# A gated linear attention with an MLP on one core: seven block products for eight in the last eight chunks, one mask instruction per visit, fewer TensorE waits, and a new instruction order

## The chip, the cores and the metric

The kernel runs on one core of a Trainium2 chip. The metric is the device time of one execution in microseconds (us); lower is better. The engines named below are PE (TensorE matmuls; PEld is its weight load), DVE (VectorE), ACT (ScalarE), POOL (GpSimd) and SP (SyncE, which issues every DMA here).

## What is computed

The attention part is a recurrence over 768 tokens for 4 batches and 8 heads of width 48. Its state is a 48x48 complex matrix per head, turned and damped at every token. The MLP takes the 3072 tokens of width 384 (8 heads by 48) through 2048 features with a parametric ReLU and back to 384.

```python
mag = np.sqrt(a_re * a_re + a_im * a_im)
scale = np.minimum(mag, 0.999) / (mag + 1e-06)
a_re_n, a_im_n = (a_re * scale, a_im * scale)
for t in range(S):
    new_re = ar * S_re - ai * S_im
    new_im = ar * S_im + ai * S_re
    kv = np.einsum('bhd,bhe->bhde', k[:, :, t], v[:, :, t])
    S_re, S_im = (new_re + kv, new_im)
    y[:, :, t] = np.einsum('bhd,bhde->bhe', q[:, :, t], S_re)
...
h = x @ w_in
g = np.maximum(h, 0.0) + alpha * np.minimum(h, 0.0)
return (g @ w_out).astype(np.float32)
```

All arithmetic that matters here is fp32. The two weight matrices arrive as 64-bit words and are turned into fp32 on the chip.

## The kernel before, in words

**Chunks and units.** The tokens are cut into 24 chunks of 128 (6 per batch). One chunk of attention is a *unit* (`unit`). For each unit the 8 heads are handled together, with 96 partitions (48 values, real and imaginary).

**Gates.** `gates` turns a_re and a_im into what the units need: the decays (`decs` in DRAM, read back as the tile `T`) and the phases (`phs` in DRAM, read back as `PP`). The phases are a running complex product over tokens, done in three levels: wide products of 8 steps (lines L338 and L340 with 576 and 288 elements), a block level with 72 and 36 elements, and a serial scan over blocks (12 and 6 elements), which starts from a `carry` of the group before. The narrow instructions (80 elements or less, and the ones after the scan, L396 to L411) run on `tiny_engine`: DVE for batch 0, GpSimd for the others. The last step spreads the scan's results over all tokens (L426 and L429 on DVE), and then the phases are sent. There are nine gate groups: chunk 0; chunks 1 and 2; chunks 3 to 5 of batch 0; and two groups of three chunks for each other batch. Three chunks make instructions of 1152 elements on 128 partitions.

**A unit.** DVE turns keys and queries by the phases (L661, L663). Then come three *visits* of two levels each, (1, 2), (4, 8) and (16, 32). At each level DVE scales one half by the decays (L717, "KQ step"), ACT copies what the next level will overwrite (L740, L756), PE forms key-query products of 32x32 blocks in PSUM (`ps_lv`, L678, 16 matmuls per level), and the products are masked into the tiles `A1` to `A32` (DVE at L702 for levels 1, 2, 4 and 8, one instruction per level; ACT at L699 for 16 and 32). After the visits PE transposes the keys (L785), forms the key-value sums (`ps_kv`, L797), multiplies the masked products by the values (`ps_y`, L817), and adds the part that comes from the state (L841). DVE carries the state on (L826, L829). ACT copies the output out, and it goes through DRAM (`ysc`) to become `xT`, the MLP's input.

**The MLP.** Chunks are taken in 14 groups of 1, 1, 2 (ten times), 1 and 1 chunks. `features` makes 128 of the 2048 features (16 rounds, f) for a group: 3 matmuls into one of two `ps_h` buffers (L889; 256 moving columns for two chunks, 128 for one), ACT's negated ReLU (L896), then one DVE instruction that joins the slopes (L898); that instruction frees the `ps_h` buffer. `outputs` multiplies a chunk's 128 features by 128 rows of w_out (L908, 384 moving columns, 16 matmuls per chunk accumulated in `ps_o`), ACT copies the sum out (L918), and SP stores it.

**The weights.** 16 pieces are loaded and converted by ACT, POOL (L515) and DVE (L517, L519) in the first part of the run.

**The order.** Every engine takes its instructions in program order, and the program order is written out by hand: `ORDER` is a string of letters, each of which lets one task (a gate group, a unit, the loads, the MLP) run to its next `yield`. The letters A to I are the gate groups, then come the loads, the weights, the 24 units, the loads of `xT` and the MLP. The numbers inside the `yield`s are costs that the writer of the string used; at run time they do nothing. Waits between engines are semaphores that the framework places from the tiles that are written and read.

## Time and profile before

| | us |
|---|---|
| median of 3 runs | 838.61 (837.79 to 839.77) |
| the profiled execution | 836.36 |
| its span, first to last instruction | 834.6 |
| PE busy | 695.8 |
| DVE busy | 651.7 |
| ACT busy | 438.7 |
| POOL busy | 200.6 |

The profile's table of stages gives for each stretch of the span the busy time of each engine, with the number of records in brackets. An fp32 matmul leaves two records, so 768 records at L908 are 384 matmuls. "Busy" of PE counts overlapping records once. The granted clock in such a table is TensorE's, as a share of full speed. The groups table gives, for a line, engine and shape, the number of records, the busy time, and the mean duration of one in ns.

### The profile page before, as it was taken

The page shows a single profiled execution, that of the slowest core. Times are in us where ns is not written, and L with a number is a line of the kernel's source. Part 1 is how long each engine was busy: PE and PEld are TensorE (multiplying, and loading weights), DVE is VectorE, ACT ScalarE, POOL GpSimd, SP SyncE. Part 2 cuts the span into 40 slices and gives each one's busy share as a digit, 9 for nine tenths or more (in the row PEclk, how much of TensorE's full clock was granted, in tenths as well). Part 3 has the DMA queues.
Part 4 walks back from the last instruction along what each step waited for, and adds up shares of the span by engine and source line. Part 5 has one row for each costly group of instructions (what it writes and reads, how often), then busy time and mean ns, then how long its engine had stood idle before and what let it go on. Part 6 is the DMA issues. An engine that isn't in the chain of part 4 may idle for free.

```text
span 834.6 us, 26848 instructions
## 1 busy us (share of the span) xinstructions
PE 695.8 (83%) x11488; PEld 527.7 (63%) x11488; DVE 651.7 (78%) x1020; ACT 438.7 (53%) x937; POOL 200.6 (24%) x293
## 2 busy tenths in 40 slices
PE   0001435889998999899999999999999999999998
PEld 0001424667776777677777777777777777777776
DVE  5989999999997899889988988979767652644112
ACT  7758787467635665565657446644344342323221
POOL 5231222328603600360135103330341000000000
PEclk9999755899999999999999999999999999999999
DMA  6696977786478579737873586457834832511110
GB/s 195 189 280 157 274 170 227 217 220 175 100 222 209 145 171 248 186 88 197 233 194 77 158 259 159 115 143 216 210 99 118 202 70 61 136 34 43 35 30 10
DMA packets 194174, 130.91 MB, mean 157 GB/s; under 512 B 74120, under 2 KB 185864, under 8 KB 194056
## 3 DMA queue, kind: packets, MB, share of 16 engines
q1 hardware_dynamic: 194056, 129.20, 58.8%
q8 instruction: 90, 1.47, 0.7%
q14 instruction: 28, 0.23, 0.1%
HBM read 100.82 MB, written 35.71 MB: 164 GB/s over the span
## 4 chain that ended last, share of the span: by engine, by line
PE 53%; DVE 23%; DMA 12%; POOL 4%; issue 4%; ACT 4%; SPq 1%; DVEq 0%; ACTq 0%; POOLq 0%
PE ps_o L908 22%; PE ps_h L889 20%; DVE KQ L717 4%; DMA T<-decs 4%; PE ps_lv L678 4%; DVE gate L426 3%; DVE gate L338 2%; PE ps_y L817 2%; DMA phs<-gate 2%; PE ps_y L841 2%; PE ps_kv L797 2%; DVE gate L429 2%; DMA g_sb<-in_w_out_dram 1%; POOL gate L338 1%; DVE gate L340 1%
## 5 line engine op out<-in xcount | busy, mean ns | idle before, releaser
L889 PE MATMUL ps_h<-xT,w_in_sb 128*128 128x256 f32 (+1 forms) x1344 | 297.3, 355 | 9.0 <-DMA xT<-ysc 7.0
L908 PE MATMUL ps_o<-w_out_sb,g_sb 128*128 128x384 f32 x768 | 297.2, 500 | 7.9 <-DVE g_sb L898 4.5
L889 PEld LDWEIGHTS ps_h<-xT,w_in_sb 128*128 128x128 f32 x1344 | 235.7, 194 | 82.1 <-DMA xT<-ysc 7.8
L898 DVE SCALAR_TENSOR_TENSOR g_sb<-g_sb,al,ps_h 128x256 f32<-128x256 f32 (+1 forms) x224 | 97.5, 436 | 117.9 <-ACT g_sb L896 117.6
L896 ACT ACTIVATE g_sb<-ps_h 128x256 f32<-128x256 f32 (+1 forms) x224 | 78.8, 352 | 200.7 <-PE ps_h L889 199.4
L908 PEld LDWEIGHTS ps_o<-w_out_sb,g_sb 128*128 128x128 f32 x768 | 136.5, 191 | 59.4 <-DVE g_sb L898 7.0
L717 DVE TENSOR_TENSOR KQ<-KQ,T 96x1024 f32<-96x1024 f32 x120 | 149.2, 1246 | 23.8 <-PE ps_lv L678 15.2
L678 PE MATMUL ps_lv<-WQ 96*32 96x32 f32 x2304 | 34.3, 204 | 72.6 <-DVE WQ L661 56.2
L678 PEld LDWEIGHTS ps_lv<-WQ 96*32 96x32 f32 x2304 | 26.5, 116 | 92.7 <-DVE WQ L661 56.2
L740 ACT COPY WQ<-KQ 96x1024 f32<-96x1024 f32 x48 | 49.9, 1040 | 22.2 <-DVE KQ L717 22.2
L338 POOL TENSOR_TENSOR gate<-gate 128x72 f32<-128x72 f32 x42 | 25.8, 615 | 134.3 <-ACT gate L368 131.5
L515 POOL TENSOR_SCALAR top<-top 128x768 f32<-128x768 f32 x16 | 41.2, 2578 | 65.2 <-ACT top L507 65.1
L756 ACT COPY W<-KQ 96x512 f32<-96x512 f32 x48 | 30.9, 644 | 40.1 <-DVE KQ L717 30.3
L338 DVE TENSOR_TENSOR gate<-gate 128x576 f32<-128x576 f32 (+5 forms) x84 | 48.6, 579 | 3.8 <-ACT gate L368 2.4
L855 ACT COPY T<-ps_y 48x256 f32<-48x256 f32 x96 | 31.6, 365 | 34.5 <-PE ps_y L841 33.7
L817 PE MATMUL ps_y<-A,VL 64*48 64x64 f32 x2304 | 42.0, 224 | 4.4 <-issue 3.8
L426 DVE TENSOR_TENSOR gate<-gate 128x1152 f32<-128x1152 f32 (+2 forms) x36 | 43.6, 1235 | 0.1
L817 PEld LDWEIGHTS ps_y<-A,VL 64*48 64x48 f32 x2304 | 39.7, 125 | 5.4 <-issue 4.5
L699 ACT ACTIVATE A<-ps_lv,columns 128x64 f32<-128x64 f32 x144 | 37.6, 334 | 9.2 <-PE ps_lv L678 9.1
L678 PE MATMUL ps_lv<-KQ,W 96*32 96x32 f32 x1536 | 24.5, 203 | 20.3 <-ACT W L756 19.7
L702 DVE TENSOR_TENSOR A<-ps_lv,mask 128x256 f32<-128x256 f32 x96 | 37.6, 412 | 0.0
L717 DVE TENSOR_TENSOR KQ<-WQ,T 96x1024 f32<-96x1024 f32 x24 | 29.5, 1231 | 6.4 <-DMA T<-decs 4.2
(106 smaller groups left out, 899.4 us busy)
## 6 DMA issues: line engine op xcount, KB each, us to landing
T<-decs SPq DMA_DIRECT2D x48, 384.0 KB
PP<-phs SPq DMA_DIRECT2D x24, 387.0 KB
KQ<-in_q_dram SPq DMA_DIRECT2D x48, 192.0 KB
decs<-gate SPq DMA_DIRECT2D x7, 1152.0 KB
phs<-gate SPq DMA_DIRECT2D x14, 576.0 KB
KQ<-in_k_dram SPq DMA_DIRECT2D x40, 192.0 KB
vsc<-in_v_dram SPq DMA_DIRECT2D x48, 144.0 KB
VL<-vsc SPq DMA_DIRECT2D x24, 288.0 KB
```

What stands on the lines that cost most here:

```text
L338: on(4 * k).tensor_tensor(out=m, in0=w[:, 1::-1].unsqueeze(2).to_broadcast([P, 2, 2, k]), in1=pairs_of(u), op=ALU.mult)
L426: TT(out=m[:, a], in0=U5[:, 1 + a], in1=turned(off3, o)[:, a].unsqueeze(1).unsqueeze(3).to_broadcast([P, L // 2, nb, 2]), op=ALU.mult)
L515: nc.gpsimd.tensor_scalar(out=top, in0=top, scalar1=F64_SMALL, scalar2=None, op0=ALU.max)
L678: nc.tensor.matmul(t[64 * i + j:64 * i + j + HC // 2, p], lhsT=keys(n, g), rhs=queries(n, g), start=True, stop=True)
L699: nc.scalar.activation(a[:, :, cols], t[:, :, at:at + name], AF.Copy, scale=s)
L717: nc.vector.tensor_tensor(out=x, in0=x if x0 is None else x0, in1=m, op=ALU.mult)
L740: nc.scalar.copy(z.rearrange("p i n t -> p i (n t)").rearrange("p i (m h) -> p m i h", h=h), bass.AP(tensor=KQ.tensor, offset=KQ.offset + ...
L817: nc.tensor.matmul(o, lhsT=Vp[h][64 * i:64 * i + 64, s, e_ * D:(e_ + 1) * D], rhs=a, start=False, stop=False)
L889: nc.tensor.matmul(p, lhsT=w_in_sb[:, f // 2, kk, f % 2 * P:(f % 2 + 1) * P], rhs=x_of[m][:, kk], start=(kk == 0), stop=(kk == NK - 1))
L896: nc.scalar.activation(gt, p, AF.Relu, scale=-1.0)
L898: nc.vector.scalar_tensor_tensor(out=gt, in0=gt, scalar=al_1[:, f:f + 1], in1=p, op0=ALU.mult, op1=ALU.add)
L908: nc.tensor.matmul(sums[0], lhsT=gt[:, c * P:(c + 1) * P], rhs=w_out_sb[:, f], start=(f == 0), stop=(f == NF - 1))
```

## The change

Six things are changed at once.

1. **Gate groups.** Batch 0 has two groups of three chunks instead of three groups (1, 2 and 3 chunks); and only the very first group keeps its narrow instructions on DVE. Those of chunks 3 to 5 move to GpSimd.
2. **Masks.** The masks of two levels lie side by side, and one DVE instruction of 512 elements per visit replaces two of 256. The tiles of levels 4 and 8 have one buffer instead of two.
3. **Waits.** The PSUM tiles `misc` and `lv` are allocated once and handed round by hand, and matmuls that read KQ or T, or write these tiles, are declared free of dependency on the loads of KQ and T. In the built program PE waits for 775 semaphores instead of 888.
4. **Output products.** For the last eight chunks, in four pairs, the product of features (2 chunks by 2048) and w_out (2048 by 384) is cut into 2x2 blocks and formed from 7 block products instead of 8. Each product is a *group* of 8 matmuls with 192 moving columns. The extra work is sums of blocks of w_out, made once (`more`: 8 DVE instructions of 768 elements), sums of blocks of features (per pair `sides`: 6 DVE instructions, and `fourth`: 2, of 512 elements), and the joining of the seven results (`plus`: 7 DVE instructions of 192 elements per pair, and one ACT copy). ACT's 16 copies of 384 elements at L918 fall away for these chunks. Space comes from the two gate buffers after the gates are done. The last pair is made of the last two groups of one chunk each.
5. **MLP order.** Features of the last five groups are interleaved with these groups of matmuls instead of with `outputs`.
6. **ORDER** is another string.

```diff
-    "AABAMMAAAAAAAAAAAAAAAAAMAAAAAMABJMNAJNNABNAAAAAAAAAAAAANKJKAKBKNBAABAAAABABBJAAAALAAAAAAABAMAAAAOKAK"
+    "AAAAAAALALLALABAAABJAMIAIIIMAMMAAALKLJAMAALAMMKKNAAAJANAAAAJANAAAAAAAJJAJAAJMMAJAAAJNNNAJNNAAAAJALAN"
...
+    def turned(i):
+        tc.declare_no_dep(i.ins, group="load", reason="the engine that this waits for has written all of it since")
...
-        tiny, tiny_engine = (DVE, nc.vector) if b == 0 else (POOL, nc.gpsimd)
+        tiny, tiny_engine = (DVE, nc.vector) if g == 0 else (POOL, nc.gpsimd)
...
+        def mask_both(name, t, e):
+            e = yield DVE(2 * HP * HC, e, takes=(R[name],))
+            a = work.tile([P, 2, HP, HC], F32, tag=f"A{name}", name=f"A{name}", bufs=2 if name == 1 else 1)
+            k = LEVELS.index(name)
+            whole = [P, 2, HP, 2, HC // 2]
+            nc.vector.tensor_tensor(out=a.rearrange("p a n (g t) -> p a n g t", g=2), in0=t.unsqueeze(3).to_broadcast(whole),
+                                    in1=both_masks[:, k:k + 2].rearrange("p a (g t) -> p a g t", g=2).unsqueeze(2).to_broadcast(whole),
+                                    op=ALU.mult)
...
+    def more():
+        T1, T2, T4 = [z[:, i * n:(i + 1) * n].rearrange("p (f e) -> p f e", f=NH) for i in range(3)]
+        held["T"] = [B11, T2, B12, T4, B21, T1, B22]
+        for dst, a, b in ((T1, B12, B11), (T2, B22, T1), (T4, B21, T2)):
+            for f in range(0, NH, 4):
+                nc.vector.tensor_tensor(out=dst[:, f:f + 4], in0=a[:, f:f + 4], in1=b[:, f:f + 4], op=ALU.subtract)
...
+    def sides(m, r):
+        A11, S2, A21, A22, A12, S1, _ = held[m]
+        for dst, a, b, op in ((S1, A21, A22, ALU.add), (A21, A11, A21, ALU.subtract), (S2, S1, A11, ALU.subtract)):
+            for f in range(0, NH, 4):
+                r = yield DVE(4 * P, r)
+                nc.vector.tensor_tensor(out=dst[:, f:f + 4], in0=a[:, f:f + 4], in1=b[:, f:f + 4], op=op)
+        return r
...
+    def group(m, j, r, tag="o"):
+        for k in range(NH):
+            nc.tensor.matmul(z, lhsT=held[m][j][:, k], rhs=held["T"][j][:, k], start=k == 0, stop=k == NH - 1)
...
+    def plus(dst, z, u, *e, takes=()):
+        t = yield DVE(DH, *e, takes=takes)
+        nc.vector.scalar_tensor_tensor(out=dst, in0=z, scalar=scale, in1=u, op0=ALU.mult, op1=ALU.add)
...
+        if alone:
+            yield from second()
+            yield "need", m + 1, NF - 1
+        r = yield from sides(m, made[m + alone, NF - 1][1])
+        yield "pause"
+        z, e = yield from group(m, 1, [t1, r], o)
+        t2 = yield from plus(u2, z, u1, e, t1)
...
-    GATES = [(0, 0, 1), (0, 1, 3), (0, 3, 6)] + [(b, c, c + 3) for b in range(1, B) for c in (0, 3)]
+    GATES = [(0, 0, 3), (0, 3, 6)] + [(b, c, c + 3) for b in range(1, B) for c in (0, 3)]
```

In the diff, `alone` is true for the last pair.

## The prediction, made before the changed kernel had run

> **What bounds the kernel now.** I read the table of stages first (start:end, length, busy time of PE, PEld, DVE, ACT and POOL, granted clock, share of the DMA engines, GB/s):

> ```profile
> 0.00:60.00 60.00, 0.66 (x32) 0.52 (x32) 46.59 (x138) 39.34 (x62) 24.60 (x38) 1.00 0.79 218
> 60.00:180.00 120.00, 59.20 (x1394) 48.27 (x1395) 117.96 (x189) 88.09 (x143) 30.94 (x17) 0.76 0.79 214
> 180.00:400.00 220.00, 206.95 (x3754) 157.16 (x3753) 200.36 (x275) 127.51 (x287) 77.24 (x119) 0.99 0.69 175
> 400.00:800.00 400.00, 397.91 (x6138) 298.46 (x6137) 279.49 (x400) 176.63 (x424) 67.84 (x119) 1.00 0.51 132
> ```

> Two kernels in one: up to 180 us DVE has no gap (118 of 120 us) while PE is half idle; from 400 us PE has none (398 of 400). Between them both are nearly full. So an edit to DVE counts early, by letting units end sooner, and an edit to PE counts late. Then PE's waits up to 180 us (who waits for whom: total, times, longest), to see what PE lacks early:

> ```profile
> PE ps_lv L678 <- DVE WQ L661: 56.2, 1, 56.2
> PE ps_lv L678 <- ACT W L756: 17.9, 6, 4.8
> PE ps_lv L678 <- ACT WQ L740: 15.9, 4, 4.8
> PE ps_kt L785 <- DVE KQ L717: 7.9, 2, 4.0
> ```

> It is the chain DVE, ACT, PE inside each unit; from 400 us PE's listed waits are 1.6 us in all. Third, the timeline's end, for the prices of the tail:

> ```profile
> 828.69 0.83 PE L889 MATMUL ps_h<-xT,w_in_sb 128*128 128x128 f32 x6
> ...
> 829.55 0.28 ACT L896 ACTIVATE g_sb<-ps_h 128x128 f32<-128x128 f32 x1 [1.04 <-PE ps_h L889]
> 829.87 0.35 DVE L898 SCALAR_TENSOR_TENSOR g_sb<-g_sb,al,ps_h 128x128 f32<-128x128 f32 x1 [0.97 <-ACT g_sb L896]
> 830.27 0.30 PEld L908 LDWEIGHTS ps_o<-w_out_sb,g_sb 128*128 128x128 f32 x2 [0.72 <-DVE g_sb L898]
> ```

> From a feature round's first matmul to the next use of its buffer: 1.68 us (828.69 to 830.37). PE's prices in steady running, from the same timeline and the chain of waits: three matmuls of 128 columns 0.67 us (0.222 each), three of 256 1.29 (0.43), two of 384 1.29 (0.645).

> **The products (PE, last 200 us).** 128 matmuls of 384 columns go: 128 x 0.645 = 82.6 us. 224 of 192 columns come. 192 is not in the trace, but the three shapes lie on a line (0.222, 0.43, 0.645), which gives 0.328: 73.5 us. **-9.1 us**; bounds -10.3 (in proportion to columns) to -7.5 (0.335). The nearest rows themselves, 0.222 and 0.43, are far apart, but the line through three points excludes both.

> DVE pays for it: 8 instructions of 768 elements at 0.95 us, 32 of 512 at 0.68 (between 0.577 for 384 elements, L826, and 0.752 for 576, L338), 28 of 192 at some 0.4 (L898: 0.34 for 128, 0.47 for 256): 41 us. From 640 us on DVE is busy 82 of 195 us, so it hides, if PE has other work while a pair's six sums (6 x 0.68 = 4.1 us) run. In the built order features and unit matmuls lie there for the first three pairs. I charge **+1 us**; uncovered it would be 4.1 us for each of three pairs, and below nothing it can't be.

> **The tail.** For the last pair the built order has 14 rounds of 128-column features with no other PE work between them, then the six sums, then 40 of the 192-column matmuls. (a) With two `ps_h` buffers a round takes 1.68 / 2 = 0.84 us against 0.67: 14 x 0.17 = **+2.4 us**. (b) After the last feature PE stands until five of six sums are done (its first wait is on the fifth): 0.86 us through ACT and DVE, 5 x 0.68, 0.1: **+4.4 us** (3.7 to 4.7 by the two rows above). (c) The clock. Around the one long late PE gap (2.12 us, for `xT`) the stages are:

> ```profile
> 262.90:266.30 3.40, 1.29 (x5) 0.60 (x4) 3.12 (x5) 2.00 (x3) 0.00 (x0) 1.00 1.16 247
> 266.30:269.80 3.50, 3.49 (x8) 2.65 (x9) 1.35 (x2) 0.38 (x1) 0.00 (x0) 0.51 0.34 63
> 269.80:273.20 3.40, 3.40 (x138) 2.66 (x137) 2.40 (x4) 2.95 (x8) 1.22 (x5) 1.00 0.29 87
> ```

> A window of 3.4 us with PE busy 38% is followed by one at half clock. A 4.4 us gap must do the same, and 2.4 to 3.4 us of the matmuls after it run at half speed: **+1.5 us** (1.2 to 1.7). [...] The end itself (a 192-element join for the 384-element copy of 0.49 us) is worth nothing. Tail: **+8.3 us**. So the products by themselves hardly pay.

> **The front (DVE).** I add, in the built order of both kernels, the mean durations of all DVE instructions ahead of a point, less 0.055 us each for the overlap of neighbours (708 us summed against 652 busy in 1020 instructions). Ahead of the last KQ step of units 1, 3, 8 and 12: before 69.6, 134.9, 266.9, 376.4; after 71.3, 128.9, 251.2, 357.4. The 19 us less at unit 12 are some 15.5 from the gates (two small groups' instructions become one: 0.56 + 0.95 against 1.35 us, and so on for each; the scan of chunks 3 to 5 goes to GpSimd), 1.7 from the masks (two of 0.412 us become one, some 0.7 by 256 more elements), and the rest from four features that come later. In the trace the last KQ steps end at 83.9, 148.6, 290.3 and 408.9: 14, 14, 23 and 33 us behind the sums.

> Start: with three chunks in the first group nothing else covers its chain between ACT and DVE. Walking it with the 1152-element rows (ACT 1.16 to 1.25, DVE 1.35; loads done by 7 us, phases sent at 58, back as PP at 66) unit 1's first instruction starts near 69.8 us against 54.9: 18.6 us behind the sum, so unit 1's last KQ step falls at 90 (before 83.9) and unit 2's at 118 (116.6).

> GpSimd: the second group's narrow steps start near 95 us. In the trace that stage lasts 29 to 46 us a group (33.2 for the first, 189.7 to 222.9), and three weight instructions (2.58 each) stand between: ready near 136. DVE comes to the spreading step at 131 and waits, with everything behind it. GpSimd's instructions there are of two lengths:

> ```profile
> 193.81 1.18 POOL L338 TENSOR_TENSOR gate<-gate 128x72 f32<-128x72 f32 x1
> ...
> 195.40 0.32 POOL L338 TENSOR_TENSOR gate<-gate 128x72 f32<-128x72 f32 x1
> ```

> [...] I charge 4 us (0 with all at the short length, 14 with the longest stage). The lag is then 22.6 us.

> Unit 12 thus ends by DVE at 357.4 + 22.6 + 10 (last KQ step to unit's end, 408.9 to 418.8) = 390. By PE: unit 8 ends near 287 (251.2 + 22.6 + 11 by DVE); up to unit 12's end the order then holds 58 output matmuls (37.4 us), 87 of 256 columns (37.4) and four units at 7.4 us (PE's 398 us from 400 to 800 less the MLP's matmuls, over 12.5 units): 391. With a few us of waits 394, against 418.8. But 6 output and 9 feature matmuls (7.7 us) that lay ahead of that point come later: **-17 us**, bounds -25 to 0. From there PE is full in both, and a lead stays to the end.

> **Fewer waits on PE.** 113 of 888 go, nearly all long satisfied. PE's idle put down to "issue" is 8.9 us in the whole trace: bounds 0 and -8.9, I take **-1 us**, nearer to nothing, since from 400 us that idle is 0.5 us. No wait is added there.

> **Sum.** -17 - 9.1 + 8.3 + 1 - 1 = -17.8 us. On the profiled execution (836.36) 818.6; the median of the runs is 2.2 us higher, so 838.61 - 17.8 = **821 us**.

> **Rivals.**
> - *A, GpSimd late.* The longest stage (46 us) with the weights between makes DVE wait 14 us instead of 4: **831**. For it: 1.12 to 1.50 us instructions beside a full DVE. Against: DVE waited for GpSimd nowhere before.
> - *B, transfers set the front: slower.* Units come sooner only if their decays and phases do. Place: T and PP of the first units. The DMA share is 1.05 at 40 to 60 us and 0.98 at 80 to 100, T<-decs takes 6.0 and 7.6 us on the chain of waits, and DVE stands in order behind a late T. If each of the first four units waits one such transfer (7.5 us), the lead of 17 turns to a loss of 13: **851**. It makes the kernel slower from 18 us of such waits on. Against: DVE's waits for DMA from 60 to 400 us are 3.6 us now, and no bytes are added.
> - *C, all goes well.* No wait for GpSimd (4), and half of the tail's cost goes because other work stands beside the sums after all: 821 - 4 - 4 = **813**.
> - *D, seven for eight doesn't pay at all.* Each of three earlier pairs stops PE for its sums (4.1 us) and drops the clock (1.5): 821 + 17 - 1 = **837**. Against: features stand beside the sums in the built order.

> **Chances.** Forecast 0.52, C 0.15, A 0.12, D 0.08, B 0.13. Within 0.2% (836.9 to 840.3, about what a measurement can tell from no change) lies most of D; faster 0.80, same 0.07, slower 0.13. The range runs from below C to above D, 809 to 842, with B outside; it takes in a front gain anywhere between 0 and 25 us.

> **What would show it.** Right: unit 1's first DVE instruction near 70 us; unit 8's end near 287 and unit 12's near 394; no PE gap over 1 us from 400 us to the tail; then one of 4 to 5 us before the last 40 matmuls, with the clock at half just after; 192-column matmuls at 0.33 us. Wrong: DVE waiting for T, PP or GpSimd for over 15 us before 200 us (A, B); PE gaps after 600 us behind the sums (D); the half clock, 54.6 us long from 95.7 us in the trace, lasting past 160 us.

## The result and the profile after

The changed kernel takes **850.08 us** (median of 4 runs, 849.68 to 850.50) against 838.20 us before (834.16 to 839.77): a ratio of 1.0149, 95% interval 1.0113 to 1.0186. It is 1.5% slower; 821 us was forecast. The profiled execution took 850.25 us with a span of 848.5 us (before: 836.36 and 834.6). In this document a run more than 1.5% above the fastest of its kernel counts as slow and is left out of times and ratios, which concerns two of the four runs of before_pad144 alone.

The table of stages of the changed kernel, with the columns of the table shown before (start:end, length, PE, PEld, DVE, ACT, POOL, granted clock, DMA share, GB/s):

```profile
0.00:60.00 60.00, 0.00 (x0) 0.00 (x0) 45.70 (x91) 41.24 (x46) 21.98 (x36) 1.00 0.75 220
60.00:180.00 120.00, 53.60 (x1298) 43.29 (x1299) 103.18 (x130) 80.96 (x130) 74.19 (x55) 0.84 0.77 210
180.00:400.00 220.00, 204.22 (x3829) 154.00 (x3828) 204.52 (x263) 131.22 (x286) 92.68 (x122) 0.98 0.67 176
400.00:800.00 400.00, 391.51 (x6287) 316.06 (x6286) 302.22 (x427) 176.10 (x426) 76.60 (x116) 1.00 0.50 132
```

Up to 180 us DVE is no longer full (103 of 120 us; 118 before), and from 400 to 800 us PE has 8.5 us of gaps where it had 2. PE's waits from 60 to 180 us, and DVE's up to 180 us (who waits for whom: total, times, longest):

```profile
PE ps_lv L691 <- DVE WQ L674: 73.9, 1, 73.9
...
PE ps_lv L691 <- ACT W L774: 13.9, 4, 5.4
...
PE ps_lv L691 <- ACT WQ L758: 10.0, 4, 2.8
```

```profile
DVE top L528 <- POOL top L526: 9.6, 4, 3.4
DVE gate L270 <- ACT gate L268: 7.3, 1, 7.3
DVE gate L312 <- ACT gate L292: 3.6, 1, 3.6
DVE gate L280 <- ACT gate L278: 3.3, 1, 3.3
```

PE starts at 73.9 us (56.2 before). DVE waits 14 us in the chain of the first gate group (before, 7.6 us at the places of L270 and L280), then 9.6 us for GpSimd, at the weight steps, for which it did not wait before.

**The 14 us of the two profiled spans, on PE.** I add PE's records in each trace: gaps, the half of its busy time in stretches with the clock at 0.5 (what full clock would have saved: in the changed kernel's trace consecutive records of 192 columns start 0.320 us apart in the median at clock 0.5 and 0.163 at 1.0), and the rest at full clock.

| us | before | after | change |
|---|---|---|---|
| ahead of the first matmul | 56.2 | 73.9 | +17.7 |
| gaps up to 400 us that an engine or a transfer ends | 68.6 | 56.9 | -11.7 |
| gaps that the profile puts down to "issue" | 8.9 | 15.2 | +6.3 |
| other gaps after 400 us | 1.7 | 9.0 | +7.3 |
| lost to half clock | 16.0 | 14.5 | -1.5 |
| output products (384 and 192 columns) | 258.6 | 248.6 | -10.0 |
| features of 128 columns | 45.5 | 48.8 | +3.3 |
| all else | 375.7 | 378.3 | +2.6 |
| end of the last matmul | 831.2 | 845.2 | +14.0 |

The products bring their 10 us. The start costs 17.7 us, and only 11.7 of them come back. The third line I had not looked at. The longest such gap, in the timeline (start, length, ..., in brackets the idle time before it and what ended it):

```profile
331.69 0.63 PE L839 MATMUL ps_y<-A,VL 64*48 64x64 f32 x32
...
332.24 0.19 PEld L986 LDWEIGHTS ps_o<-w_out_sb,g_sb 128*128 128x128 f32 x1
...
336.77 2.08 PE L986 MATMUL ps_o<-w_out_sb,g_sb 128*128 128x384 f32 x3 [4.46 <-issue]
```

Nothing in the profile releases it, and a weight load of the same product had run at 332.24 us. I number PE's records (matmuls, weight loads and its semaphore waits) in order: this gap stands ahead of number 8130 = 31 x 256 + 194. The one at 167.6 us stands at 2498 = 9 x 256 + 194, the two longest of before at 2 x 256 + 195 and 32 x 256 + 194. In all 19 traces of this study there are 171 unexplained gaps of over 0.25 us on PE, and every one stands at numbers 194 to 196 of a block of 256. (Why at 194 and not at 0 is not shown; some 62 instructions ahead of the first record would do it.) The profiles count the transfers of instructions (before, then after: packets, MB, share):

```profile
q8 instruction: 90, 1.47, 0.7%
```

```profile
q8 instruction: 92, 1.51, 0.7%
```

23217 records make 90.7 blocks of 256, 23518 make 91.9; a packet is 1.51 MB / 92 = 16.4 kB, 64 bytes for each of 256 instructions. The times of these packets settle it. One lands at 335.47 us and the gap above ends at 336.77; one lands at 170.94 and the gap from 167.6 us ends at 172.36. Each of the 171 gaps ends 1.2 to 1.8 us after such a packet has landed. So PE waits for the next block of its program.

### The profile page after: what moved, and what is told of

Read it like the earlier page. It is cut to its first block, busy times and chain, and to the rows that moved or that the text cites. A ratio compares the mean times of both kernels' runs of the same rounds, so it can differ in the third digit from the quotient of the medians.

```text
span 848.5 us, 27088 instructions
## 1 busy us (share of the span) xinstructions
PE 690.2 (81%) x11680; PEld 552.6 (65%) x11680; DVE 671.2 (79%) x947; ACT 436.0 (51%) x910; POOL 265.5 (31%) x329
## 3 DMA queue, kind: packets, MB, share of 16 engines
q8 instruction: 92, 1.51, 0.7%
## 4 chain that ended last, share of the span: by engine, by line
PE 52%; DVE 16%; POOL 11%; DMA 6%; ACT 6%; issue 5%; SPq 3%; DVEq 0%; ACTq 0%; POOLq 0%
PE ps_h L952 20%; PE ps_o L986 12%; PE ps_o L1056 8%; PE ps_lv L691 3%; DVE KQ L735 3%; POOL gate L349 3%; PE ps_y L839 2%; POOL run L351 2%; DVE gate L437 2%; PE ps_y L865 2%; DMA T<-decs 2%; POOL gate L351 2%; PE ps_misc L819 1%; SPq L637 1%; PE ps_misc L807 1%
## 5 line engine op out<-in xcount | busy, mean ns | idle before, releaser
L986 PE MATMUL ps_o<-w_out_sb,g_sb 128*128 128x384 f32 x512 | 201.6, 508 | 13.9 <-DVE g_sb L969 6.7
L967 ACT ACTIVATE g_sb<-ps_h 128x256 f32<-128x256 f32 (+1 forms) x176 | 63.9, 363 | 139.8 <-PE ps_h L952 138.8
L986 PEld LDWEIGHTS ps_o<-w_out_sb,g_sb 128*128 128x128 f32 x512 | 91.7, 193 | 50.8 <-DVE g_sb L969 8.5
L969 DVE SCALAR_TENSOR_TENSOR g_sb<-g_sb,al,ps_h 128x256 f32<-128x256 f32 (+1 forms) x176 | 78.6, 448 | 51.9 <-ACT g_sb L967 51.5
L691 PE MATMUL ps_lv<-WQ 96*32 96x32 f32 x2304 | 34.5, 203 | 85.2 <-DVE WQ L674 73.9
L691 PEld LDWEIGHTS ps_lv<-WQ 96*32 96x32 f32 x2304 | 26.5, 115 | 103.3 <-DVE WQ L674 73.9
L526 POOL TENSOR_SCALAR top<-top 128x768 f32<-128x768 f32 x16 | 39.3, 2462 | 35.1 <-ACT top L518 35.1
L329 POOL TENSOR_TENSOR gate<-gate 128x72 f32<-128x72 f32 (+2 forms) x21 | 26.9, 1282 | 64.8 <-DVE gate L329 63.7
L967 ACT ACTIVATE gate<-ps_h 128x128 f32<-128x128 f32 (+1 forms) x48 | 15.0, 312 | 59.6 <-PE ps_h L952 59.6
L349 DVE TENSOR_TENSOR gate<-gate 128x576 f32<-128x576 f32 (+1 forms) x63 | 44.8, 711 | 1.0
L969 DVE SCALAR_TENSOR_TENSOR gate<-gate,al,ps_h 128x128 f32<-128x128 f32 (+1 forms) x48 | 18.7, 390 | 33.4 <-ACT gate L967 33.2
L437 DVE TENSOR_TENSOR gate<-gate 128x1152 f32<-128x1152 f32 x32 | 43.4, 1390 | 0.4 <-POOL gate L422 0.3
L349 POOL TENSOR_TENSOR gate<-run,runs 128x12 f32<-128x12 f32 x42 | 29.0, 690 | 38.6 <-ACT runs L379 35.8
```

Source lines behind the costliest of these rows:

```text
L349: on(4 * k).tensor_tensor(out=m, in0=w[:, 1::-1].unsqueeze(2).to_broadcast([P, 2, 2, k]), in1=pairs_of(u), op=ALU.mult)
L437: TT(out=m[:, a], in0=U5[:, 1 + a], in1=turned(off3, o)[:, a].unsqueeze(1).unsqueeze(3).to_broadcast([P, L // 2, nb, 2]), op=ALU.mult)
L526: nc.gpsimd.tensor_scalar(out=top, in0=top, scalar1=F64_SMALL, scalar2=None, op0=ALU.max)
L691: turned(nc.tensor.matmul(t[64 * i + j:64 * i + j + HC // 2, p], lhsT=keys(n, g), rhs=queries(n, g), start=True, stop=True))
L967: nc.scalar.activation(gt, p, AF.Relu, scale=-1.0)
L969: nc.vector.scalar_tensor_tensor(out=gt, in0=gt, scalar=al_1[:, f:f + 1], in1=p, op0=ALU.mult, op1=ALU.add)
```

## Experiments

Each chip ran the kernel before beside the others; ratios are to those runs. "Gaps" are the unexplained gaps at block bounds in the one profiled execution of the kernel, us. They differ between executions of one program: 15.2 in the first profile of the changed kernel, 18.5 in after_again. The profiled execution can also lie at the edge of its runs: 853.2 us for tail_order (median 846.6), 868.8 for eight_products (865.4).

| kernel | us | ratio (95%) | gaps |
|---|---|---|---|
| old_front | 887.7 | 1.0568 (1.0517 to 1.0619) | 20.7 |
| eight_products | 865.4 | 1.0293 (1.0236 to 1.0350) | 20.4 |
| tail_order | 846.6 | 1.0081 (1.0045 to 1.0116) | 18.7 |
| old_front_tail | 879.2 | 1.0470 (1.0409 to 1.0531) | 17.5 |
| after_again | 856.0 | 1.0187 (1.0128 to 1.0246) | 18.5 |
| after_pad232 | 842.8 | 1.0018 (0.9992 to 1.0044) | 5.0 |
| after_pad64 | 870.2 | 1.0364 (1.0317 to 1.0410) | 35.1 |
| before_pad144 | 865.4 and 877.3 | 871.3 / 841.2 = 1.036, no interval | 32.5 |
| tail_pad232 | 835.4 | 0.9945 (0.9921 to 0.9970) | 5.8 |
| tiny_dve_pad232 | 843.3 | 1.0042 (1.0019 to 1.0064) | 9.6 |
| eight_pad232 | 850.6 | 1.0123 (1.0085 to 1.0161) | 9.5 |
| tail_again | 834.7 | 0.9931 (0.9906 to 0.9956) | 8.4 |
| old_start_tail | 837.6 | 0.9973 (0.9951 to 0.9995) | 7.5 |
| masks_split | 835.4 | 0.9940 (0.9910 to 0.9970) | 8.0 |
| weights_dve | 830.4 | 0.9885 (0.9848 to 0.9921) | 11.6 |
| waits_back | 843.7 | 1.0029 (0.9991 to 1.0067) | 14.6 |

### Parts undone

My theory F: the loss is in the front. Its rival P: the products.

**old_front**: gate groups and written order of before.

```diff
-    GATES = [(0, 0, 3), (0, 3, 6)] + [(b, c, c + 3) for b in range(1, B) for c in (0, 3)]
+    GATES = [(0, 0, 1), (0, 1, 3), (0, 3, 6)] + [(b, c, c + 3) for b in range(1, B) for c in (0, 3)]
-        tiny, tiny_engine = (DVE, nc.vector) if g == 0 else (POOL, nc.gpsimd)
+        tiny, tiny_engine = (DVE, nc.vector) if b == 0 else (POOL, nc.gpsimd)
```

> The changed kernel (seven products, one mask operation per visit, fewer waits) with the gate groups and the written order of the kernel before; the steps of the product groups stand where the output steps stood. Theory F (the time went in the front: three chunks in the first gate group start TensorE 17.7 us later, the second group's narrow steps on GpSimd hold up the weight steps, and the 19 us that VectorE saves are eaten by its waits; the products, -10.0 us, are paid back by the tail, +8.9): TensorE starts near 56 us again, its idle time up to 400 us returns from 142 to about 133 us, and the time is 835 to 840 us. Rival P (the seven products and their sums cost the time, through VectorE and through waits of TensorE after 500 us): 846 to 851 us, with TensorE idle over 5 us between 500 and 700 us.

887.7 us: F's time fell, and P's too. PE's idle time up to 400 us came back to 132.5 us as F said, but 41.7 us of gaps came after 400 us (2.2 in before): 10 us for `xT`, 8 for sums, 7 for ACT's copies to `W`, 11 at block bounds. The old order was written for the old code; with other instruction lengths behind it, it seems to be a bad order (argued, not tested by itself). So swapping orders did not undo this part.

**eight_products**: the features and outputs of before in the new order (`all_mlp` of before, `more` left out).

> The changed kernel with the eight block products of the kernel before in the last eight chunks (no sums, no weight differences); gates, order, masks and waits as changed. Theory F: 850.1 + 10.0 (products) - 8.9 (gap of 3.85, half clock 1.5 and slow feature rounds 3.2 in the tail, rounded) = 851 us, 849 to 853; the idle time up to 400 us stays at 142 us. Rival P: most of the 12 us come back, 838 to 842 us.

865.4 us, not 851. Against tail_order on the same chip that is 19 us, where F allowed 9.5.

**tail_order**: the last pair reordered.

```diff
-            if k == 3 and (m != LAST or j in (0, 4)):
+            if (m == LAST and j in (0, 4)) or (k == 3 and m != LAST):
                 yield "pause"
...
+            z3, e3 = yield from group(m, 3, r0, o)
             r = yield from sides(m, r0)
+            z5, e5 = yield from group(m, 5, r, lv)
             z, e = yield from group(m, 1, [t1, r], misc)
```

> The changed kernel with another order of the last pair alone: its first two product groups are spread one matmul to a feature round, and behind the last feature comes first the group that needs no sums, then the one that needs two of the six, then the others. My theory of the tail: the gap of 3.85 us before the last 40 matmuls, the half clock behind it (1.5 us) and the slow feature rounds (3.2 us) go: 850.1 - 8.5 = 841.5 us, 840 to 844, and the granted clock stays at 1 after 790 us. Rival: ScalarE and VectorE set the pace of the last features, so only the gap goes: 845 to 847 us.

846.6 us, above the theory's range and inside the rival's (845 to 847), but the rival's mechanism, that only the gap goes, is not what the trace shows. In its trace the gap and the half clock after 790 us are gone, as expected, and the features of 128 columns take 47.0 us (48.8); from unit 24's end to the last matmul it is 43.5 us (50.8). But unit 24 ended 10 us later than in the changed kernel's profile, with 18.7 us of gaps at block bounds. (Two profiles of the changed kernel itself, 850.2 and 858.6 us, differ there by 8 us.)

**old_front_tail**: both edits.

> Both of the above together: gate groups and order of the kernel before, seven products, and the new order of the last pair. Theory F: 837.5 - 8.5 = 829 us, 826 to 832, which is faster than both kernels. Rival P: 838 to 843 us.

879.2 us: the tail's gain of 8.5 us shows again (887.7 to 879.2), on a base that F had wrong.

All four of theory F's times were off, and in all four kernels the gaps at block bounds come to 17 to 21 us. That made them the suspect (theory C).

### The bounds of the instruction blocks alone

Tiny matmuls ahead of everything, in the time in which PE waits for the first unit anyway. They shift every later instruction against the bounds and leave the order and every other engine's program as they were (116 matmuls: 4.8 us of 67). They hardly act through the granted clock either: up to 160 us half clock costs 5.8 us in the changed kernel, 6.0 with 116 tiny matmuls and 7.2 with 32.

```diff
+    pads = ps.tile([P, MT], F32, tag="h", name="ps_pad", bufs=2)
+    low = ident.bitcast(BF16)
+    for _ in range(116):
+        nc.tensor.matmul(pads[0:48, 0:16], lhsT=low[0:64, 0:48], rhs=low[0:64, 0:16], start=True, stop=True)
+
     with tc.manual_schedule():
```

32 matmuls in after_pad64, and 72 in before_pad144, on the kernel before.

> The changed kernel once more, unaltered, as the base for the other three on the same chip: 848 to 852 us, TensorE's unexplained gaps (those the trace puts down to issue) at the same places of the program as in its first profile, 15 us in all.

> The changed kernel with 116 tiny matmuls (232 instructions for TensorE, a few us in all) ahead of everything, in the 74 us in which TensorE has nothing to do; their output is never read. Theory C (code loading): TensorE's unexplained gaps stand in all six traces so far at the 194th of each 256 of its instructions, and almost only where the 256 before were through in under 5 us, so they are waits for the next block of instructions. The padding shifts the bounds of the blocks by 232; counted from the trace of the changed kernel, the blocks then miss a mark of 5 us by 21 us in all, against 36 now, and at the 0.42 to 0.6 us of gap for each us of this that the six traces show the gaps fall from 15 to 9 to 12 us, with some half clock behind them gone: 841 to 846 us. Rival S (the gaps are some other engine's lateness, at those places by chance, or the order alone makes the difference): within 1 us of the unpadded kernel.

> The same with 32 tiny matmuls (64 instructions): the blocks then miss the mark of 5 us by 61 us in all. Theory C: gaps of 26 to 35 us, with half clock behind the long ones, 862 to 875 us. Rival S: within 1 us of the unpadded kernel.

> The kernel before with 72 tiny matmuls (144 instructions) ahead of everything. In its trace the blocks miss the mark of 5 us by 18 us in all, the least of all shifts by multiples of 8; shifted by 144 they miss it by 64, the most. Theory C: gaps of 27 to 38 us instead of 9, with half clock behind the long ones, 858 to 875 us, slower than the changed kernel, although nothing but the place of the bounds is altered. Rival S: 838 us, within 1 us of the kernel before.

Theory C holds in both directions. The same program takes 842.8, 856.0 or 870.2 us, with 5.0, 18.5 and 35.1 us of gaps; and the kernel before, shifted by 144 instructions, takes 865.4 and 877.3 us instead of 841.2, more than the unpadded changed kernel. Not all of the figures held: the unpadded kernel came out at 856.0 us, not 848 to 852, and the gaps of after_pad232 at 5.0, not 9 to 12. PE's waits put down to "issue" in after_pad64, in before_pad144 and in after_pad232 (total, times, longest):

```profile
PE ps_y L839 <- issue: 21.4, 12, 4.1
...
PE ps_y L865 <- issue: 8.8, 6, 2.0
...
PE ps_lv L691 <- issue: 4.9, 4, 1.6
```

```profile
PE ps_y L817 <- issue: 18.0, 12, 2.2
...
PE ps_lv L678 <- issue: 8.0, 5, 3.4
...
PE ps_y L841 <- issue: 6.5, 3, 3.2
```

```profile
PE ps_h L952 <- issue: 2.7, 1, 2.7
```

With the bad paddings they sit in `ps_y` and `ps_lv`, the shortest matmuls (0.20 to 0.23 us a record in the mean in the changed kernel's trace, against 0.28 to 0.51 in the MLP): the key-value sums, the local products and the state's part of a unit are some 390 instructions there, in 3.7 to 4.2 us where none of them waits. The half clock adds to the gaps: after 160 us 21.5 us are lost to it in before_pad144, 3.4 in the profile of before.

### With the gaps small: what the parts are worth

**tail_pad232** is tail_order with the 116 matmuls, **eight_pad232** is eight_products with them, **tiny_dve_pad232** is after_pad232 with the narrow steps of chunks 3 to 5 on VectorE (`b == 0` in place of `g == 0`).

> The changed kernel with the new order of the last pair (as in tail_order) and the 232 padding instructions (as in after_pad232). Theory C and my theory of the tail add up: 842.8 us of after_pad232 less 3.85 (gap), 1.5 (half clock) and 2 to 3 (feature rounds) = 835 us, 833 to 838, some 0.7% faster than the kernel before on the same chip. Rival: what the tail saves comes back as waits for instruction blocks or at the end: 840 to 843 us.

> The changed kernel with 232 padding instructions, and the narrow steps of the second gate group on VectorE, as before the change, not on GpSimd. Theory G (GpSimd's share of the front is a wash): VectorE's waits of 9.6 us for the weight steps of GpSimd up to 132 us go, and some 10 us of narrow steps come to VectorE (7 x 0.31 + 7 x 0.18 + 6 x 0.22 + 6 x 0.16 and the wider ones, by their rows in the trace of before): 840 to 845 us. Rival: GpSimd's lateness is what ate the front, and unit 12 ends 8 us or more earlier: 832 to 836 us.

> The changed kernel with eight block products in place of seven, and 232 padding instructions, which suit its blocks as well (21 us missed against 33 without). Theory C: with the waits for instruction blocks out of the way the products show what they are worth: ends less those waits and less the half clock behind them were 831 us with eight products and 821 to 823 with seven, so 842.8 + 9 = 852 us, 849 to 855. Rival (first forecast, products paid back by the tail): 842 to 845 us.

All three came out in their forecast ranges: 835.4, 843.3 and 850.6 us. tail_pad232 is faster than both kernels (0.9945 of before), and again as tail_again (0.9931).

**load_probe**: 768 tiny matmuls ahead and 768 behind.

> The changed kernel with 768 tiny matmuls (1536 instructions, six blocks of 256) ahead of everything, while TensorE is idle and transfers run at 0.7 to 1.0 of the DMA engines, and 768 more behind everything, when hardly a transfer runs. The time is not to be compared. Theory C: at each bound a gap, and the time of a block with its gap is the time to load the next: 4 to 8 us each at the start, 2.5 to 3.5 at the end, as in the stalls of the other traces. Rival (the load takes no longer under transfers): the same at both ends.

Half an answer; the gap at each bound did not come. A block of tiny matmuls takes 5.1 us by itself, so only loads of over 5.1 us show: of the first bounds two did, with 7.3 and 5.9 us for block and gap (at 21 and 29 us, in 5 us stretches with DMA shares of 0.68 and 0.65 right behind one of 1.11), none at the end, where the share is 0.02 to 0.04. So loads of over 5.1 us occur under transfers and were not seen without them; but two blocks entered between 5 and 15 us, at shares of 1.03 and 1.12, had no gap behind them, and how fast a load is without transfers this run doesn't say.

### What holds the loss of the rest

eight_pad232 has the products of before and about its gaps (9.5 against 8.9 us), and is 10.8 us slower than the kernel before on its chip (850.64 - 839.79). The rest of the change had been forecast at -18 us. I took this loss to lie in the front; the two profiles say otherwise. At the end of unit 8 (its last matmul on PE) eight_pad232 is 4.5 us late (305.1 against 300.6 us) with the same matmuls of the MLP done. At the end of unit 12 it is 6.1 us early (412.7 against 418.8) with 7.8 us of them put off, so 1.7 us late. At the end of unit 24 it is 5.5 us late (804.5 against 799.0) with 8.7 us put off: 14 us. So most of the loss falls between units 12 and 24. From 400 us on PE there waits 7.5 us for engines and transfers, against 1.7 before, and some 2 us more at block bounds. Four more edits, on tail_pad232:

```diff
-        nc.gpsimd.tensor_scalar(out=top, in0=top, scalar1=F64_SMALL, scalar2=None, op0=ALU.max)
+        nc.vector.tensor_scalar(out=top, in0=top, scalar1=F64_SMALL, scalar2=None, op0=ALU.max)
```

That is weights_dve. old_start_tail has the first two gate groups and the first 298 steps of the order of before; masks_split issues the mask operation in two halves; waits_back drops the marks that take TensorE's waits out (here, and in `load` likewise):

```diff
     def turned(i):
-        tc.declare_no_dep(i.ins, group="load", reason="the engine that this waits for has written all of it since")
+        pass
```

> The kernel of tail_pad232 once more, unaltered, as the base of the other three on the same chip: 833 to 838 us.

> The base with the first two gate groups of the kernel before (one chunk, then two) and the first 298 steps of its written order; the rest as in the base, the narrow steps of both groups on VectorE, those of chunks 3 to 5 on GpSimd. Theory L (the front's saving is given back as lag: a first group of three chunks spares VectorE some 6 us of instructions and makes it wait 7 us longer, 21.4 against 14.2 behind its sum): TensorE starts near 56 us, and the time is 832 to 838 us, at most 3 off the base. Rival B1 (the late start is the loss of the front by itself): the 17.7 us of later start, or most of them, come off: 818 to 825 us.

> The base with the one mask operation of 512 elements per visit split into two of 256 again, 48 x (2 x 0.41 - 0.68) = 7 us more of VectorE, half of it up to unit 12. Theory of the forecast (VectorE's sum sets the front): 2 to 4 us slower than the base. Rival L2 (units wait for chains between engines, not for VectorE's sum): within 1.5 us of the base.

> The base with the sixteen weight steps of GpSimd (the maximum over 768 elements, 2.46 us each there) on VectorE, at some 0.6 us each (estimate from the shift on the same tile, 0.62). VectorE's 12.2 us of waits for them up to 300 us go, 9.6 us of instructions come. Theory G (GpSimd's share is a wash): within 3 us of the base. Rival (those waits ate the front): 822 to 827 us.

> The kernel of tail_pad232 with TensorE's waits back that the change had taken out (113 semaphore waits, on tiles and loads long ready; some need an instruction of their own, which also shifts the bounds of the instruction blocks a little along the program). My term for the fewer waits (-1 us): 836 us, at most 1 off the base when the gaps at the block bounds are taken off both. Rival W (the waits matter more): 3 us or more slower with those gaps taken off.

- old_start_tail: 837.6 us, 2.9 slower than the base. The units start 18 us sooner (54.96 against 72.95 us), but the last copy of unit 1's output ends 2.6 us later (120.3 against 117.7): the late start isn't what delays the units.
- masks_split: 835.4 us against 834.7, no difference that can be told from noise, and unit 12 ends at 413.1 us (413.4). But neighbouring instructions overlap (0.055 us each in the trace of before), and the masks' busy time grew by 3.1 us (32.6 to 35.7), not 7, with half of it up to unit 12. So the run fits L2 but is a weak test of whether VectorE's sum sets the front.
- weights_dve: 830.4 us, 4.3 faster, more than theory G's 3 and less than its rival's 8 to 13. VectorE's waits for the weight steps are gone from its list, and unit 12 ends at 409.7 us (413.4 in the base). It is the fastest version here: 0.9885 of before, though its gaps at block bounds are 3 to 6 us longer than the base's; with gaps and late half clock taken off, as in the next item, it gains 4.5 to 8 us.
- waits_back: 843.7 us. Ends less the gaps at bounds and less the half clock after 160 us are 816.0 us here, 818.1 and 814.4 in the two traces of the base: the waits that came back cost nothing that can be told. Counted in the traces these are only 51 of the 114 that went (786 waits on PE in the base, 837 here; 780 in the changed kernel, 894 in before), so a cost of the others is not excluded. Their 25 more records on PE move the bounds, and the gaps go from 5.8 and 8.4 us to 14.6.

So moving the weight steps off GpSimd wins back 4 of some 11 us. That the change lost these 4 through GpSimd is argued, not shown: its own move of narrow steps, taken back in tiny_dve_pad232, cut VectorE's waits for the weight steps from 9.6 to 2.0 us and gained nothing. The other 6 or 7 stay open. Waits after unit 12 hold part of them; the new written order, which wasn't taken back by itself, is the suspect left, untested.

## Why the prediction was wrong, step by step

1. **The front, forecast -17 (bounds -25 to 0): failed.** Unit 8 ended at 306.4 us (forecast 287), unit 12 at 417.1 (394; before 418.8). The step that failed is the lag of DVE behind its own sum, put at 22.6 us to unit 12. Measured at the last KQ steps it was 23.5 us at unit 1, 32.1 at unit 3, 39.6 at unit 8 and 49.5 at unit 12. By the prediction's own reckoning (unit 12's end, and 7.7 us of matmuls that come later) the front came out at -1.7 + 7.7 = +6 us, and with the padding of after_pad232 (unit 12 at 413.6) at +2.5. The start itself was nearly right (the first unit's first instruction near 72.6 us, forecast 69.8). No run shows the 4 us for GpSimd, which were my estimate; in their place DVE waited 9.6 us for it, and not at the spreading step but at the weight steps queued behind its narrow ones. The rest are many short waits for PE, ACT and transfers that my constant lag left out, though before's own lag had grown from 14 to 33 us between units 3 and 12. So the 19 us that DVE's sum lost were given back as waiting: 49.5 - 32.5 = 17 us more lag at unit 12. (The recorded 287 for unit 8 is 2 us more than its terms, 251.2 + 22.6 + 11, add up to.)
2. **The products, -9.1: right.** 258.6 to 248.6 us, -10.0; a 192-column matmul took 74.9 / 224 = 0.334 us (forecast 0.328).
3. **Sums hidden in the middle, +1: right.** No PE gap between 400 and 800 us waits for a sum; rival D fell. But the sign "no PE gap over 1 us from 400 us to the tail" failed: there are gaps of 1.5 and 1.7 us at block bounds, one of 2.5 for ACT's output copy and one of 1.6 for its copy to `W`.
4. **The tail, +8.3: right in each term.** (a) 2.4 forecast; the last features' joins on DVE (L969) come every 0.84 us in the mean (six steps from 821.88 to 826.93 us), the 0.84 of the forecast; (b) 4.4 forecast, 3.85 measured; (c) 1.5 forecast, half of 3.0 busy us at half clock. The lower bound of (b) should have read 3.8, and the line through the three shapes gives 0.327; neither matters. PE around it in the timeline, and the windows of the stages' table with the gap and what follows:

```profile
825.75 0.83 PE L952 MATMUL ps_h<-xT,w_in_sb 128*128 128x128 f32 x6
830.43 0.98 PE L1056 MATMUL ps_o<-gate 128*128 128x192 f32 x2 [3.85 <-DVE gate L1019]
```

```profile
826.60:830.00 3.40, 0.00 (x0) 0.00 (x0) 3.08 (x7) 0.28 (x1) 0.00 (x0) 1.00 0.00 0
830.00:833.40 3.40, 2.96 (x9) 3.00 (x10) 0.89 (x2) 0.00 (x0) 0.00 (x0) 0.51 0.00 0
833.40:836.80 3.40, 3.40 (x22) 3.40 (x22) 1.56 (x3) 0.00 (x0) 0.00 (x0) 0.99 0.00 0
```

   Reordered, it gave back 1.0018 - 0.9945 = 0.7%, some 6 us.
5. **Fewer waits, -1: nothing that the runs show.** Here lies the error that turned a draw into a loss. I read the 8.9 us of PE's "issue" as a cost that fewer waits might lower, and asked no further. They were waits for instruction blocks, and the new program lay worse against the bounds: 15.2 us, and 5.4 us lost to half clock right behind the two longest (half of 5.73 and of 5.16 busy us). With the bounds shifted the kernel stands at 1.0018 of before instead of 1.0149 to 1.0187: this term, which no line of the sum had, is worth 11 to 14 us.

With that term aside the change is a draw: seven products with their tail as built bring 1.0123 - 1.0018 = 1.05%, 9 us, and the rest of the change, forecast at -18 us, loses some 11, most of them behind unit 12. Rival B gave the right time, 851 us, for a wrong reason: DVE's waits for transfers up to 180 us are 0.3 us. Rival A named the right engine.

## What to carry to other kernels

Where a profile shows a long engine program with gaps that nothing releases, number the instructions: if the gaps stand at multiples of one block size (256 here), a comparison of two versions measures their alignment too, here by 27 us of 840 for one program and some 30 for another. Judge an edit at two or three paddings before believing it. A saving in an engine's sum counts only where that engine, and not the chain between engines, ends the waits: of the 19 us that DVE's sum lost here, 17 came back as lag. A lag that grows in the trace of before (14 to 33 us here) is not to be carried on as a constant.
